# Loading q and k six rows to a partition for three batches, holding the last batch's loads back, and a new order of work

## The chip, the cores and the metric

The kernel runs on one core of one Trainium2 chip. The core has a matrix engine (TensorE, "PE" in the profile, with its weight loads as "PEld"), a vector engine (VectorE, "DVE"), a scalar engine (ScalarE, "ACT"), a general engine (GpSimd, "POOL"), a sync engine ("SP") that here only issues DMA transfers, and 16 DMA engines that all queues share. The metric is the device time of one execution in microseconds; less is better.

## The reference

The inputs are q, k, v of 4 batches, 8 heads, 768 positions and 64 columns. A flag for each head says whether it is a full causal head or a streaming head, which sees only the first 4 positions and the last 64. Then come two projections, an elementwise maximum, and a third projection.

```python
scores = scale * np.matmul(q, k.transpose(0, 1, 3, 2))
mask = np.where(retr[0, :, 0, 0, None, None], full_mask, stream_mask)
a = np.exp(scores - max); a = a / (np.sum(a, axis=-1, keepdims=True) + 1e-09)
x = np.matmul(a, v)  ->  (batch * position, 8 heads * 64)
g = np.maximum(x @ w1, x @ w2)          # 512 -> 1024
out = g @ w_out                          # 1024 -> 512, float32, 3072 rows
```

Three heads are full and five are streaming in this draw.

## The kernel before

**Tiling.** The work is cut into 8 halves, (batch, half), of 384 positions each. The heads are sorted by flag, and taken in four pairs ("FF", "FS", "SS", "SS"). For each half and pair, q and k are cast to bf16 (L774, copies at L523 and L525 into the tile `qb`), turned by TensorE into PSUM (L798, six transposes at L805), and copied to the tile `qk` (`unturn`, L810), where the rows get back their order. Scores are products of k and q (L1019) into pairs of PSUM banks; ScalarE takes the exponential (L1038) into `at`; VectorE multiplies the masks in (L1057), except in half (0,0), where a matrix product adds them (L988). TensorE then multiplies by v, with a column of ones for the sum (L1082), and `normalise` (L1090) divides (L1099, L1109) into `x`.

**The projections.** The maximum of two products is written as relu(x·(w1 − w2))·w_out + x·(w2·w_out). So before the first half can be projected, VectorE forms w1 − w2 (L1238), TensorE turns w2 (L1254) and multiplies it by w_out (L1272) into `w2o`. This needs all three weights on the chip. After that each half has 32 products at L1293, the relu at L1317 or L1319, and 36 products at L1343 into the output rows (more and narrower ones in the last tile); they are copied out (L523, L525) and stored from SP's queue (L1362).

**Loads.** Batches 0, 1 and 2 come in float32 through three slots of the tile `ld`, which batches, halves and the weights w1 and w2 take in turn; a load waits until the last reader of its slot is done. q and k of a half are one transfer each on SP's queue (L583): 128 partitions, of which each holds three consecutive rows of every head, 768 bytes a piece. v is three transfers of 128 rows (L596), in pieces of 256 bytes. The weights w1 and w2 come in two transfers each on SP's queue (L677). w_out comes in four parts on POOL's queue (L694), cast on the way, and each part is issued behind a small copy on POOL (`landed`, L693) that reads the last byte of an earlier load and so waits for it. With `PACE = 1` that is the load before the latest one in the list `LOADS`; with 0 it is the latest. `LOADS` lists the loads of batch 0 and the weights: `A` and `Av` are q with k, and v, of half (0,0), `B` and `Bv` those of (0,1), `w20` is the first half of w2, `wo0` the first quarter of w_out.

Batch 3 comes in another way: q, k and v of each head are cast by the DMA and issued from POOL (`load_pair`, L629, issues at L640), 24 transfers; q and k of a pair are then turned by a DMA transpose from SP's queue (L654).

**The order.** Each engine runs its own list of instructions in a fixed order and waits at semaphores. The lists are made when the kernel is built: the class `Order` (L133) plays the whole program through with a cost for each operation, and writes each instruction to its engine at the moment at which its play begins it. What is ready at the same time is chosen by rank (`RANK`, `FRONT`, `FRONT_STEP`, `STEP`); an operation that more than one engine can do goes where it would end first, plus a bias. TensorE takes the first ready operation by the sequence of its lists; `MARGIN` says how long an operation must have been ready before it is preferred (TQ: the transposes at L805). Until 38 us of the play, gaps on TensorE are filled with products that nobody reads (`warmer`, L513). Such a filler counts as busy in the profile. `S_AFTER` says after which pair of a half the scores of the next half may begin.

`SPLIT` names the halves whose q and k are cast, turned and copied apart ((0,0) and (0,1)). The six-row form is in the code already, and is switched off by the empty `SIX`:

```python
    def six_rows(s):
        return lds[:, s, 0:2].rearrange("p t h c -> p (t h c)").rearrange("p (h c) -> p h c", h=H)
    def rows_of(s, t):
        return six_rows(s)[64 * t:64 * t + 64]
```

Of the kernel before, what the change touches and what calls it, by code (L numbers as in the profile page):

```python
# [15 lines left out]
ACT = mybir.ActivationFunctionType  # L16
# [116 lines left out]
class Order:  # L133
# [23 lines left out]
    def pe(self, name, cost, emit, deps=(), **more):  # L157
        more.setdefault("margin", MARGIN.get(name, 0.0))
        o = self.op({"PE": cost}, emit, deps, lat=0.2, share=SHARE.get(name, 1.0), **more)
        self.lists.setdefault(name, []).append(o)  # L160
        return o
# [228 lines left out]
CAST_QK = {'POOL': 0.46, 'DVE': 0.27, 'ACT': 0.4}  # L390
CAST_V = {'POOL': 0.3, 'DVE': 0.26, 'ACT': 0.26}
RANK = {
    'cast': -1.3, 'vcast': 13.15, 'unturn': 5.85, 'mix_k': 2.0, 'mix_v': -14.6, 'exp': -3.1,
    'mask': -0.85, 'norm': -11.9, 'take_x': -1.7, 'turn': -20.3, 'w2b': -16.95, 'sub': -8.25,
    'w2t': -4.1, 'wob': -0.85, 'w2o': -5.15, 'relu': 5.25, 'load': 5.9, 'out': -10.1, 'h2': 7.5,
    'table': -10.0, 'vload': 15.45,
}
NLD = 3
NQB = 4
NQK = 8  # L400
# [7 lines left out]
PE_LISTS = ('TX', 'W', 'S', 'TK', 'TQ', 'P', 'H', 'P2', 'F')  # L408
PLACES = (0, 1, 2, 0, 1, 2, 0, 1, 2, 0, 1, 2, 0, 1, 2, 0, 1, 2, 0, 1, 2, 0)
SECOND_UP = False  # L410
LOADS = ('A', 'B', 'Av', 'wo0', 'wo1', 'w20', 'wo2', 'wo3', 'w10', 'w21', 'w11', 'Bv')
BIAS = {'DVE': 0, 'ACT': 0}
BIAS_MIX = {}
W2B_BEHIND = True
NORM = {'DVE': 0.35}
TURNED_BY_DMA = ()
DMA_TURN = 0.25
PACE = 1
W2O_EARLY = 3
X_LAST = ((0, 0),)  # L420
BIASED = ((0, 0),)
# [2 lines left out]
RING_LATE = 1.0  # L424
RING = {'SP': 3300, 'POOL': 6200, 'ACT': 4224}
SPLIT = ((0, 0), (0, 1))
SIX = ()
K_BY_ACT = False
LAST_BY_ACT = True
K_LANDS = 7.6  # L430
# [6 lines left out]
    0.22, 'six': 0.37,  # L437
}
SPARE = {}
STEP = 0.2  # L440
FF_STEP = -7.9
S_AFTER = 1
S_RUN = 2
S_REST = 1
ENTER_S = 0.1
# [2 lines left out]
COLD_UNTIL = 7.5  # L448
WARM_SHARE = 0.9
SHARE = {'S': 0.45, 'W': 0.8}  # L450
MARGIN = {'W': 0.5, 'S': 2.0, 'F': 2.0, 'TQ': 2.0}
X_MARGIN = 0.4
FRONT = (
    {'mix_k': -17.5, 'mask': 49.1, 'unturn': -40.9, 'exp': 20.1, 'vcast': 23.1, 'cast': -83.2,
    'norm': 5.9}, {'vcast': 14.2, 'unturn': -4.2, 'exp': 54.0, 'mask': 18.5, 'norm': -6.2,
    'mix_k': 18.4, 'cast': 15.9},
)
FRONT_STEP = (36.1, 8.2)
UNTURN_BIAS = ({'ACT': 0.5}, {'ACT': 0.5})
SHARED = 0.89  # L460
UP_PARTS = 2
BY_ACT = {}
V_QUEUES = ()


def tile_three_full_heads(
# [3 lines left out]
    nc = tc.nc  # L470
    B, H, S, D = q.shape
    HALF = S // 2
    NT = HALF // 128
# [13 lines left out]
    w2b = keep.tile([128, KC, d_ff], BF16, name="w2b")  # L487
    w12 = keep.tile([128, KC, d_ff], BF16, name="w12")
    w2t = keep.tile([128, FC, d_model], BF16, name="w2t")
    w2o = keep.tile([128, KC, d_model], BF16, name="w2o")  # L490
    wob = keep.tile([128, FC, d_model], BF16, name="wob")
# [11 lines left out]
    landed = keep.tile([128, 1], F32, name="landed")  # L503
# [15 lines left out]
    T = {}  # L519
# [7 lines left out]
    def rank_of(kind, b, hf, at=0):  # L527
        if b:
            return RANK[kind]
        return RANK[kind] + FRONT[hf].get(kind, 0.0) + FRONT_STEP[hf] * at  # L530

# [17 lines left out]
    number, freed, loads, later, asked = [0], {}, {}, [], []  # L549
# [20 lines left out]
    def load_half(b, hf, kinds=(0, 1, 2)):  # L570
# [4 lines left out]
        def whole(t, src):  # L575
            six = (b, hf) in SIX

# [46 lines left out]
    def staged(n):  # L624
        a = lds[:, slot_of[n // HP, 0]].rearrange("p t h c -> p (t h c)").bitcast(BF16)
        a = a.rearrange("p (g c) -> p g c", c=1536)[:, n % HP]
        return a.rearrange("p (i t h d) -> p i t h d", t=2, h=2, d=D)

    def load_pair(b, p):  # L629

        n = b * HP + p
        if p == 0:
            slot_of[b, 0], old, tenants[b] = slot()
            staged_old[b] = old
        got = {}
        for hh in range(2):
            for t, src in enumerate((q, k, v)):
                def emit(_, t=t, src=src, hh=hh):
                    to = vbs[:, n % NQK, hh, :, 0:D] if t == 2 else staged(n)[:, :, t, hh]
                    nc.gpsimd.dma_start(  # L640
                        out=to,
                        in_=src[b, bass.ds(heads[2 * p + hh], 1)].rearrange("o (i p) d -> p (o i) d", p=128),
                    )
                o = op(
                    {"POOL": CAST_ISSUE}, emit,
                    [*last_w.get(n - NQK, ())] if t == 2 else [first_w[b - 2, 1, p], *wo_in.values()],
                    data=0.197 / RATE["cast"], rank=RANK["load"], parts=768, tag=f"load{b}.{p}", port=("POOL",),
                )
                if t < 2:
                    later.append((o, staged_old[b]))  # L650
                got[t, hh] = o

        def turn_pair(_):
            nc.sync.dma_start_transpose(  # L654
                out=qks[:, n % NQK].rearrange("f t (i c) -> f (t i) c", c=128),
                in_=staged(n).rearrange("p i t h d -> p (i t h d)"),
            )
        un = op(
            {"SP": 1.7}, turn_pair, [got[t, hh] for t in range(2) for hh in range(2)] + list(last_s.get(n - NQK, ())),
            data=DMA_TURN * 4 * NT, tag=f"turn{b}.{p}", rank=RANK["turn"],  # L660
        )
        leaves(b, range(3), [un])
        return un, [got[2, 0], got[2, 1]]
# [39 lines left out]
    slot_of, tenants, bias_in, table_in, staged_old, half_old, place_of = {}, {}, [], [], {}, {}, {}  # L703
    w1_in, w2_in, wo_in, flow = {}, {}, {}, []
    for what in LOADS:
        kind, c = what[:2], int(what[2:]) if what[:1] == "w" else 0
        if what[0] in "ABCD":
# [4 lines left out]
            for n, o in enumerate(loads[(*of, kinds[-1])]):  # L712
                last = (n if kinds[-1] == 2 or of not in LONG else NT - 1) * D
                row = 64 if kinds[-1] == 1 and of in SIX else 0
                place_of[o] = row, lds[row:row + 1, slot_of[of], kinds[-1], 0, last:last + 1]
        elif kind == "wo":
            wo_in[c] = load_down(c, flow[-1 - PACE:len(flow) - PACE])
        else:
# [29 lines left out]
    last_turn, last_s, last_w = {}, {}, {}  # L748
# [21 lines left out]
    def cast_qk(n, hf, hh, lo=0, hi=2):  # L770
        b, p = first_half(n)

        def emit(e):
            if (b, hf) in SIX:  # L774
                src = six_rows(slot_of[b, hf])[:, bass.ds(heads[2 * p + hh], 1), :]
# [34 lines left out]
    def unturn(n, hf, lo=0, hi=2):  # L810
        def emit(e):
            if (n // HP, hf) in SIX:
                src = bank(("pt", n, hf, 0), BF16)[:, 0:2 * HALF]
# [66 lines left out]
    def prepare(b, hf, p):  # L880
# [7 lines left out]
        else:  # L888
# [4 lines left out]
            for hh in range(2):  # L893
                for lo, hi in ((0, 1), (1, 2)) if (b, hf) in SPLIT and (b, hf) not in SIX else ((0, 2),):
                    cs.append(cast := op(
                        dict(CAST_QK) if hi - lo == 2 else dict(CAST_V), cast_qk(n, hf, hh, lo, hi),
                        [*(o for t in range(lo, hi) for o in loads[b, hf, t]), registers, *old_qb],
                        tag=f"cast{b}.{hf}.{p}", rank=rank_of("cast", b, hf, p), port=("DVE", "POOL"),
                        bias=BIAS if b else None,
                    ))  # L900
# [8 lines left out]
            for hh in range(2) if b not in V_BY_DMA else ():  # L909
                vs.append(op(  # L910
                    dict(CAST_V), cast_v(n, hf, hh), [*loads[b, hf, 2], registers, *old_v],
                    tag=f"vcast{b}.{hf}.{p}", rank=rank_of("vcast", b, hf, p), port=("POOL", "DVE"), bias=BIAS if b else None,
                ))
# [9 lines left out]
            else:  # L923
                last_turn[n, hf], turned[n, hf] = [], []
                tq = None
                for lo, hi in ((0, 1), (1, 2)) if (b, hf) in SPLIT else ((0, 2),):
                    if tq is not None and (b, hf) in SIX:
                        un = op(
                            {"DVE": 0.08 + 0.41, "ACT": 0.065 + 0.325}, unturn(n, hf, lo, hi), [tq, *old_s],
                            frees=[key], tag=f"unturn{b}.{hf}.{p}", rank=rank_of("unturn", b, hf, p),  # L930
                            bias=None if b else UNTURN_BIAS[hf],
                        )
# [15 lines left out]
                        tag=f"unturn{b}.{hf}.{p}", rank=rank_of("unturn", b, hf, p),  # L948
                        bias=None if b else UNTURN_BIAS[hf],
                    )  # L950
# [166 lines left out]
    first_w = {}  # L1117
    x_ready, norms, x_free, xt_free, at_users, all_exps = {}, {}, {}, {}, [], {}

    def attend(b, hf):  # L1120
        group = group_of(b, hf)
        exps, done = {}, {}
        for t in range(len(group)):
# [13 lines left out]
            if b or hf:  # L1137
                deps.append(first_w[(b, 0, S_AFTER) if hf else (b - 1, 1, S_AFTER)])
            s = pe("S", cost, scores(b, hf, t), deps, claims=[(("ps", b, hf, t), 2)], tag=("S", b, hf, t))
# [25 lines left out]
        for t in range(len(group)):  # L1165
            for p in range(HP):
# [13 lines left out]
                if last:  # L1180
                    old = x_free.get(len(x_free) - NX, ())
                    r = op({"DVE": 0.12}, normalise(b, hf, p, 0), [w], tag=f"norm{b}.{hf}.{p}", rank=rank_of("norm", b, hf, p))
                    a = op(dict(NORM), normalise(b, hf, p, 1), [r, *old], tag=f"norm{b}.{hf}.{p}", rank=rank_of("norm", b, hf, p))
                    z = op(
                        dict(NORM), normalise(b, hf, p, 2), [r, *old],
                        frees=[("po", n, hf)], tag=f"norm{b}.{hf}.{p}", rank=rank_of("norm", b, hf, p),
# [112 lines left out]
    def forward(b, hf, x_deps, sub_ops, wob_ops, w2o_ops):  # L1299
        old_g = g_free.get(len(g_free) - NG, ())  # L1300
        order.shift = STEP * (2 * b + hf) + FF_STEP
        relus, users = [], []
# [75 lines left out]
    for b in range(B):  # L1378
        for hf in range(2):
# [3 lines left out]
            if b and b not in CAST_BY_DMA:  # L1383
                load_half(b, hf, [t for t in range(3) if (b, hf, t) not in loads])
            order.shift = STEP * (2 * b + hf)
            for p in range(HP):
# [3 lines left out]
            if (b, hf) > (0, 1):  # L1390
                b0, hf0 = (b, 0) if hf else (b - 1, 1)
                forward(b0, hf0, x_ready[b0, hf0], *weights)
            order.shift = STEP * (2 * b + hf)
            attend(b, hf)
# [31 lines left out]
    o = pe("P", 0.06, total, [j], claims=[("judge", 1)], margin=8.0)  # L1426
# [327 lines left out]
```

## Time and profile before

| | |
|---|---|
| median of 3 runs | 183.98 us (183.62 to 185.08) |
| profiled execution | 183.75 us |
| its span, first to last instruction | 182.1 us |
| PE busy | 173.6 us, of which fillers (L513) 13.8 |
| ACT, DVE, POOL busy | 133.9, 100.9, 41.0 us |
| moved by DMA | 32.37 MB, 178 GB/s in the mean |

The profile comes from one execution. A row of a group gives line, engine, operation, tiles and shapes, the count, then busy us and mean ns of one, then the idle time before it and what ended that. A row of the timeline or of the chain of waits begins with the start and the length in us. A row of a table by stretches gives the stretch, its length, the busy time of each engine with its count of instructions, the granted clock of TensorE, the DMA engines' share (which can pass 1.00 where packets overlap) and GB/s. Busy PE time includes pipelined overlap, so it is not PE at its peak.

### The profile page before, as it was taken

What the parts mean: (1) busy time and instruction counts of PE and PEld (TensorE: products, weight loads), DVE (VectorE), ACT (ScalarE), POOL (GpSimd) and SP (SyncE); (2) the same over time, 40 slices, a digit from 0 to 9 for tenths busy, and PEclk for the clock granted to TensorE, in tenths of its full rate; (3) what the DMA queues carried; (4) which work ended last, traced back from release to release, by engine and by line L of the source; (5) the groups of instructions that cost most, each with busy time, mean ns of one, the idle gap of its engine ahead of it and who ended that gap; (6) DMA issues with size and microseconds to landing.
All of it is one profiled execution on the core that took longest, in us unless ns stands there. A gap on an engine that the chain in (4) does not pass through costs nothing.

```text
span 182.1 us, 5021 instructions
## 1 busy us (share of the span) xinstructions
PE 173.6 (95%) x1847; PEld 107.4 (59%) x1847; DVE 100.9 (55%) x303; ACT 133.9 (74%) x295; POOL 41.0 (23%) x80
## 2 busy tenths in 40 slices
PE   7998999999998999999978999999999999999992
PEld 7955974566655757655634676455566545545561
DVE  5678984698698996739444778734467300000000
ACT  3688996588599899999689999569796614624421
POOL 6414400041105905907693000000000000000000
PEclk9999999999999999999999999999999999999998
DMA  4999999999999999999999999720142313012013
GB/s 129 334 305 224 359 200 327 315 273 312 207 285 285 304 217 220 221 211 209 133 176 169 173 219 147 170 93 0 41 118 107 89 58 115 11 58 115 0 61 121
DMA packets 72529, 32.37 MB, mean 178 GB/s; under 512 B 53938, under 2 KB 67506, under 8 KB 72498
## 3 DMA queue, kind: packets, MB, share of 16 engines
q1 hardware_dynamic: 52448, 28.45, 63.8%
q0 software_dynamic: 19904, 3.41, 25.2%
q8 instruction: 16, 0.26, 0.6%
q14 instruction: 15, 0.12, 0.2%
q10 hardware_dynamic: 146, 0.13, 0.2%
HBM read 25.17 MB, written 6.29 MB: 173 GB/s over the span
## 4 chain that ended last, share of the span: by engine, by line
PE 60%; DMA 18%; SPq 8%; ACT 7%; issue 3%; DVE 1%; ACTq 0%; DVEq 0%; POOL 0%
PE ps L1343 25%; PE ps L1293 18%; DMA ld<-in_v_dram 10%; PE ps L1019 6%; PE ps L1082 5%; DMA wob<-in_moe_w_out_dram 5%; SPq L596 5%; DMA ld<-in_k_dram 4%; PE ps L1272 4%; SPq L583 3%; ACT at L1038 2%; PE ps L805 1%; ACT vb L523 1%; ACT qk L523 1%; ACT ot L523 1%
## 5 line engine op out<-in xcount | busy, mean ns | idle before, releaser
L1038 ACT ACTIVATE at<-ps 128x512 bf16<-128x512 f32 (+2 forms) x134 | 63.8, 589 | 2.9 <-PE ps L1019 2.8
L1343 PE MATMUL ps<-wob,g 128*128 128x512 bf16 (+1 forms) x200 | 46.7, 371 | 0.0
L1293 PE MATMUL ps<-xt,w 128*128 128x384 bf16 x256 | 45.6, 326 | 0.2 <-DVE x L1109 0.2
L1293 PEld LDWEIGHTS <-w 128*128 128x128 bf16 x256 | 23.7, 98 | 15.6 <-issue 0.6
L1057 DVE TENSOR_TENSOR at<-at,tab 128x1024 bf16<-128x1024 bf16 (+5 forms) x49 | 24.1, 508 | 12.1 <-ACT at L1038 11.6
L523 ACT COPY ot<-ps 128x512 f32<-128x512 f32 (+1 forms) x23 | 13.4, 582 | 23.1 <-PE ps L1343 22.9
L1317 ACT ACTIVATE g<-ps 128x384 bf16<-128x384 f32 x52 | 25.6, 500 | 6.2 <-PE ps L1293 5.9
L1343 PEld LDWEIGHTS <-g 128*128 128x128 bf16 x200 | 18.3, 98 | 18.3 <-issue 0.2
L1343 PE MATMUL ps<-w2o,xt 128*128 128x512 bf16 (+1 forms) x100 | 24.8, 371 | 0.0
L1109 DVE TENSOR_TENSOR x<-ps,rez 128x192 f32 x64 | 22.8, 357 | 1.9 <-DVE rez L1099 0.3
L1082 PEld LDWEIGHTS <-at 128*128 128x128 bf16 x477 | 19.1, 97 | 6.7 <-issue 0.7
L1019 PE MATMUL ps<-qk 64*128 64x128 bf16 (+1 forms) x330 | 20.2, 228 | 2.1 <-DVE g L1319 0.8
L1082 PE MATMUL ps<-vb,at 128*128 128x65 bf16 x387 | 20.9, 193 | 0.4 <-ACT ot L523 0.4
L1019 PEld LDWEIGHTS <-qk 64*128 64x128 bf16 x330 | 12.4, 94 | 12.7 <-issue 9.7
L513 PE MATMUL ps<-warmer 128*128 128x128 bf16 x150 | 13.8, 251 | 1.2 <-POOL warmer L1687 1.2
L525 POOL CAST vb<-ld 128x192 bf16 x21 | 8.8, 455 | 26.4 <-DMA ld<-in_v_dram 25.4
L523 ACT COPY qk<-ps 128x768 bf16<-128x768 bf16 (+1 forms) x17 | 12.5, 771 | 2.9 <-PE ps L805 2.3
L1343 PEld LDWEIGHTS <-xt 128*128 128x128 bf16 x100 | 9.1, 98 | 8.7 <-issue 0.2
L513 PEld LDWEIGHTS <-warmer 128*128 128x128 bf16 x150 | 11.4, 116 | 1.4 <-POOL warmer L1687 1.2
L525 DVE CAST qb<-ld 128x384 bf16 (+1 forms) x30 | 9.5, 371 | 4.6 <-DMA ld<-in_k_dram 2.5
L805 PE MATMUL ps<-tab,qb 128*128 128x128 bf16 x144 | 11.2, 219 | 0.8 <-DVE qk L525 0.6
L805 PEld LDWEIGHTS <-qb 128*128 128x128 bf16 x144 | 9.1, 98 | 2.7 <-issue 0.9
(70 smaller groups left out, 157.8 us busy)
## 6 DMA issues: line engine op xcount, KB each, us to landing
out_dram<-ot SPq DMA_DIRECT2D x23, 256.0 KB, 2.1
ld<-in_q_dram SPq DMA_DIRECT2D x6, 768.0 KB, 7.9
ld<-in_k_dram SPq DMA_DIRECT2D x6, 768.0 KB, 8.2
ld<-in_v_dram SPq DMA_DIRECT2D x18, 256.0 KB, 7.5
ld<-in_moe_w_dram SPq DMA_DIRECT2D x4, 1024.0 KB, 13.4
wob<-in_moe_w_out_dram POOLq DMA_DIRECT2D x4, 256.0 KB, 9.9
ld<-in_q_dram POOLq DMA_DIRECT2D x8, 96.0 KB, 7.6
ld<-in_k_dram POOLq DMA_DIRECT2D x8, 96.0 KB, 9.0
```

The lines of the kernel that those rows point to most:

```text
L513: nc.tensor.matmul(banks[e][:, 0:128], lhsT=warm, rhs=warm, start=True, stop=True)
L523: nc.scalar.copy(out=out, in_=in_)
L525: eng[e].tensor_copy(out=out, in_=in_)
L805: nc.tensor.transpose(to[:, i], qbs[:, T["qb", n, hf] % NQB, t, i].rearrange("p h d -> p (h d)"), ident)
L1019: nc.tensor.matmul(to.rearrange("p (i c) -> p i c", c=128), lhsT=lhsT, rhs=q_of(n, i, m)[rows], start=bk not in under, stop=True, skip_gro ...
L1038: nc.scalar.activation(out=at[:, bk, 0:w], in_=bank(("ps", b, hf, t), part=bk)[:, 0:w], func=ACT.Exp, scale=scale,)
L1057: eng[e].tensor_tensor(out=at, in0=at, in1=tbl, op=ALU.mult)
L1082: nc.tensor.matmul(po[:, hh, i - NT * hf, :], lhsT=ats[:, T["at", b, hf, t] % NAT, bk, e * 128:(e + 1) * 128], rhs=rhs, start=first, stop= ...
L1109: nc.vector.tensor_tensor(out=xs[:, (2 * b + hf) % NX, :, bass.ds(heads[2 * p + hh], 1), :], in0=po[:, hh, :, 0:D].unsqueeze(2), in1=z[:, ...
L1293: nc.tensor.matmul(bank(key)[:, 0:HALF], lhsT=w[:, kc, fc * 128:(fc + 1) * 128], rhs=xts[:, (2 * b + hf) % NXT, :, kc, :], start=(kc == 0) ...
L1317: nc.scalar.activation(out=g, in_=ph, func=ACT.Relu)
L1343: nc.tensor.matmul(bank(key)[:, cols], lhsT=lhsT, rhs=(w2o if kind == "x" else wob)[:, c, cols], start=(e == 0), stop=(e == len(steps) - 1),)
```

## The change

q and k of both halves of batches 0, 1 and 2 are loaded six rows to a partition: q to partitions 0 to 63, k to 64 to 127, in pieces of 1536 bytes, 512 to a transfer instead of 1024. The bytes are the same. One cast of a head then covers q and k together (384 columns), in the halves (0,0) and (0,1) too, where there were two of 192; those halves' transposes wait for both, and still leave as two copies, one for q and one for k.

The loads of the last batch get a new dependency (`BEHIND`): the last piece of v of half (2,1). On the chip it is one small copy on POOL ahead of the first of the 24 issues, and what POOL has after it waits with it.

The order is made anew with other ranks, biases and allowances, another sequence of the first loads, `PACE` 0 and `S_AFTER` 3; `normalise` may also go to ScalarE.

```diff
 RANK = {
-    'cast': -1.3, 'vcast': 13.15, 'unturn': 5.85, 'mix_k': 2.0, 'mix_v': -14.6, 'exp': -3.1,
-    'mask': -0.85, 'norm': -11.9, 'take_x': -1.7, 'turn': -20.3, 'w2b': -16.95, 'sub': -8.25,
-    'w2t': -4.1, 'wob': -0.85, 'w2o': -5.15, 'relu': 5.25, 'load': 5.9, 'out': -10.1, 'h2': 7.5,
-    'table': -10.0, 'vload': 15.45,
+    'cast': 1.15, 'vcast': 15.65, 'unturn': 5.0, 'mix_k': 0.45, 'mix_v': -20.2, 'exp': -1.1,
+    'mask': -5.2, 'norm': -13.75, 'take_x': -6.45, 'turn': -23.55, 'w2b': -16.65, 'sub': -8.15,
+    'w2t': -7.35, 'wob': 1.75, 'w2o': -7.35, 'relu': 7.4, 'load': 4.95, 'out': -9.55, 'h2':
+    1.15, 'table': -14.3, 'vload': 12.0,
 }
...
-LOADS = ('A', 'B', 'Av', 'wo0', 'wo1', 'w20', 'wo2', 'wo3', 'w10', 'w21', 'w11', 'Bv')
-BIAS = {'DVE': 0, 'ACT': 0}
+LOADS = ('A', 'wo0', 'B', 'Av', 'wo1', 'wo2', 'w20', 'wo3', 'w21', 'Bv', 'w10', 'w11')
+BIAS = {'DVE': 1, 'ACT': 0.5}
...
-NORM = {'DVE': 0.35}
+NORM = {'DVE': 0.35, 'ACT': 0.6}
...
-PACE = 1
+PACE = 0
...
-SIX = ()
+SIX = ((0, 0), (0, 1), (1, 0), (1, 1), (2, 0), (2, 1))
...
-STEP = 0.2
-FF_STEP = -7.9
-S_AFTER = 1
+STEP = 0.15
+FF_STEP = -10.1
+S_AFTER = 3
...
-MARGIN = {'W': 0.5, 'S': 2.0, 'F': 2.0, 'TQ': 2.0}
+MARGIN = {'W': 0.5, 'S': 2.0, 'F': 0.5, 'TQ': 0.2}
...
-FRONT_STEP = (36.1, 8.2)
-UNTURN_BIAS = ({'ACT': 0.5}, {'ACT': 0.5})
+FRONT_STEP = (39.0, 7.4)
+UNTURN_BIAS = ({}, {'ACT': 1.0})
...
+BEHIND = (1, 2)
...
     def load_pair(b, p):
 
         n = b * HP + p
+        behind = loads[b - 1, BEHIND[0], BEHIND[1]][-1:] if BEHIND else []
+        for o in behind:
+            place_of[o] = 0, lds[0:1, slot_of[b - 1, BEHIND[0]], BEHIND[1], 0, NT * D - D:NT * D - D + 1]
...
                 def emit(_, t=t, src=src, hh=hh):
+                    for o in [] if T.get("last batch") else behind:
+                        row, place = place_of[o]
+                        nc.gpsimd.tensor_copy(out=landed[row:row + 1], in_=place)
+                    T["last batch"] = True
...
-                    [*last_w.get(n - NQK, ())] if t == 2 else [first_w[b - 2, 1, p], *wo_in.values()],
+                    [*behind, *(last_w.get(n - NQK, ()) if t == 2 else [first_w[b - 2, 1, p], *wo_in.values()])],
```

More of the change, by code (lines that the diff above doesn't have):

```diff
@@ L450 @@
 SHARE = {'S': 0.45, 'W': 0.8}
-MARGIN = {'W': 0.5, 'S': 2.0, 'F': 2.0, 'TQ': 2.0}
+MARGIN = {'W': 0.5, 'S': 2.0, 'F': 0.5, 'TQ': 0.2}
 X_MARGIN = 0.4
 FRONT = (
-    {'mix_k': -17.5, 'mask': 49.1, 'unturn': -40.9, 'exp': 20.1, 'vcast': 23.1, 'cast': -83.2,
-    'norm': 5.9}, {'vcast': 14.2, 'unturn': -4.2, 'exp': 54.0, 'mask': 18.5, 'norm': -6.2,
-    'mix_k': 18.4, 'cast': 15.9},
-)
-FRONT_STEP = (36.1, 8.2)
-UNTURN_BIAS = ({'ACT': 0.5}, {'ACT': 0.5})
+    {'mix_k': -6.2, 'mask': 52.7, 'unturn': -49.6, 'exp': 10.0, 'vcast': 24.8, 'cast': -61.4,
+    'norm': 14.4}, {'vcast': 24.4, 'unturn': -12.0, 'exp': 63.5, 'mask': 37.1, 'norm': -0.1,
+    'mix_k': 39.3, 'cast': 11.1},
+)
+FRONT_STEP = (39.0, 7.4)
+UNTURN_BIAS = ({}, {'ACT': 1.0})
 SHARED = 0.89
```

## The prediction, made before the changed kernel was seen

> **What bounds the kernel now.** I read the page's first lines, then a table by stretches whose cuts lie where TensorE's idle time lies, then the row of the fillers.
>
> ```profile
> span 182.1 us, 5021 instructions
> ...
> PE 173.6 (95%) x1847; PEld 107.4 (59%) x1847; DVE 100.9 (55%) x303; ACT 133.9 (74%) x295; POOL 41.0 (23%) x80
> ...
> L513 PE MATMUL ps<-warmer 128*128 128x128 bf16 x150 | 13.8, 251 | 1.2 <-POOL warmer L1687 1.2
> ```
> ```profile
> core 0: us, PE busy (x) PEld busy (x) DVE busy (x) ACT busy (x) POOL busy (x), PEclk, DMA share, GB/s
> 0.00:25.60 25.60, 23.36 (x348) 19.22 (x349) 19.68 (x71) 19.23 (x48) 9.87 (x30) 1.00 0.99 263
> 25.60:57.00 31.40, 31.40 (x338) 19.01 (x338) 23.11 (x58) 24.55 (x55) 4.93 (x9) 1.00 1.07 282
> 57.00:59.00 2.00, 1.16 (x15) 0.64 (x10) 1.97 (x7) 2.00 (x6) 1.27 (x5) 1.00 0.94 264
> 59.00:92.00 33.00, 32.82 (x393) 20.65 (x391) 23.43 (x69) 30.55 (x68) 19.76 (x31) 1.00 1.53 215
> 92.00:100.00 8.00, 6.18 (x70) 2.96 (x69) 4.35 (x12) 7.36 (x18) 5.21 (x7) 1.00 2.04 183
> 100.00:178.70 78.70, 78.63 (x699) 44.94 (x695) 28.34 (x89) 49.87 (x106) 0.00 (x0) 1.00 0.45 95
> 178.70:182.10 3.40, 0.00 (x0) 0.00 (x0) 0.00 (x0) 0.34 (x1) 0.00 (x0) 0.81 0.25 80
> ```
>
> TensorE bounds it. Without the 13.8 us of fillers its work is 159.8 us, which the change leaves as it is: the same transposes and products. The other 22.3 us of the span are what can move. The front holds 16.0 (13.8 of fillers, 25.60 − 23.36 = 2.2 idle). Later idle time is 0.84 at 57 to 59, 0.18 before 92, 1.82 at 92 to 100 and 0.07 after: 2.9 together. The tail after the last product is 3.4. The granted clock is 1.00 wherever PE works. So an edit pays if it brings useful work into the first 25.6 us or takes away part of the 2.9, and costs where it opens a new gap.
>
> What ends the front stands in the chain of waits and, around it, in the timeline:
>
> ```profile
> 8.45 8.19 DMA ld<-in_v_dram
> 16.64 0.05 issue
> 16.69 0.12 POOL landed L693
> 16.82 8.71 DMA wob<-in_moe_w_out_dram
> 25.52 0.04 issue
> 25.56 0.59 PE ps L1272 x2
> ```
> ```profile
> 6.03 0.87 DVE L525 CAST qb<-ld 128x192 bf16 x3 [1.05 <-DMA ld<-in_q_dram]
> ...
> 8.46 1.11 ACT L523 CAST qb<-ld 128x192 bf16 x4 [0.15 <-DMA ld<-in_k_dram]
> ...
> 22.89 1.28 DVE L525 COPY w2t<-ps 128x1024 bf16<-128x1024 bf16 x2
> ...
> 24.22 1.11 PE L513 MATMUL ps<-warmer 128*128 128x128 bf16 x17
> ```
>
> The last long gap is filled by 17 products of the warmer from 24.22, while the turned w2 is ready at 24.17 (22.89 + 1.28). What is missing is w_out, issued at 16.82 behind a piece of v. Behind this the DMA engines are full: a share of 0.99 over the whole front.
>
> **The change part by part.**
>
> *w_out earlier.* With `wo0` behind the load of k of (0,0), its issue moves from 16.82 to about 8.5, and with the same 8.71 us it lands at 17.2, before 24.17. The product at L1272 can then begin 1.3 us sooner; the fillers there are 1.11. Its second quarter still waits for v, and its bytes now compete with q and k of (0,1), so the bounds are −1.3 and 0. I take −1.1. On POOL the copy and the issue go past the casts of q and k of batch 0:
>
> ```profile
> L694 POOL DMA_DIRECT2D wob<-in_moe_w_out_dram x4 | 3.1, 771 | 0.0
> ```
>
> A cast behind them on POOL waits 0.9 us (0.12 + 0.77); DVE and ACT can take it, so 0, and 0.9 at most for one pair.
>
> *Six rows to a partition.* q is there at 6.03, k at 8.46: 2.43 us for 768 KB in pieces of 768 bytes. No row shows a piece of 1536 bytes, or a load into 64 partitions. The nearest rows are the front's loads and a stretch in which mostly weights come, in pieces of 2 KB:
>
> ```profile
> 5.00:7.50 2.50, 2.50 (x32) 2.47 (x31) 1.36 (x5) 1.47 (x6) 1.21 (x3) 1.00 1.10 332
> ...
> 30.00:32.50 2.50, 2.50 (x14) 1.10 (x12) 0.29 (x1) 1.49 (x5) 0.00 (x0) 1.00 1.06 401
> ```
>
> If long pieces are the reason for 401 against 332 GB/s, a load takes 2.43 × 332 / 401 = 2.01 us, 0.42 less. Four such loads stand ahead of v and the weights: −1.7 at best. On the other side, if half the partitions meant half the rate, each would take 4.86, +9.7 for four. I take −1.0: the packet count halves, and 1536 bytes is nearer to the second row. The other end is the first rival below.
>
> [...]
>
> *q and k cast together.*
>
> ```profile
> L525 DVE COPY qk<-ps 128x384 bf16<-128x384 bf16 x13 | 6.5, 552 | 0.8 <-PE ps L805 0.6
> ...
> L525 DVE CAST qb<-ld 128x384 bf16 x18 | 6.1, 387 | 2.3 <-DMA ld<-in_k_dram 1.5 <-DMA out_dram<-ot 0.8
> ...
> L523 ACT CAST qb<-ld 128x384 bf16 x9 | 4.4, 540 | 0.0
> L523 ACT CAST qb<-ld 128x192 bf16 x15 | 4.3, 353 | 2.5 <-DMA ld<-in_q_dram 2.4 <-DMA ld<-in_k_dram 0.2
> ...
> L525 DVE CAST qb<-ld 128x192 bf16 x12 | 3.5, 347 | 2.2 <-DMA ld<-in_q_dram 1.1 <-DMA ld<-in_k_dram 1.0
> ```
>
> Two casts of 0.35 become one of 0.39 (DVE) or 0.54 (ACT); 32 casts become 16, and 11.2 us of engine time about 7.4. Against that, q's casts and four copies of 0.55 were done between 6.03 and 8.46, while k was on its way; now they stand behind k: 2.2 us over two engines, 1.1 for the last pair, and for the first about 0.2 (a longer cast and three more transposes). Half of the 3.8 saved falls on (0,0). Net +0.2, between −1 and +1.3.
>
> *v of (0,1) ahead of w1.* Two pieces of 256 KB move ahead of w1, 1.9 us at 282 GB/s. The products at L1293 begin later, those with v of (0,1) earlier; PE has no gap in 25.60 to 57.00, so one fills for the other. 0; up to +1.9 if nothing fills it.
>
> The front sums to −1.1 − 1.0 + 0.2 + 0 = −1.9.
>
> *The last batch's loads wait.* From 60 to 100 two queues share the DMA engines: SP's, and POOL's with the loads of batch 3. Below are the queues in that stretch, then a piece of the chain, then PE's longest gap after it in the timeline:
>
> ```profile
> q1 hardware_dynamic: 14997, 6.27, 83.1%
> q0 software_dynamic: 14960, 1.88, 80.2%
> ```
> ```profile
> 78.73 9.14 DMA ld<-in_v_dram
> ```
> ```profile
> 94.88 0.29 PE L1019 MATMUL ps<-qk 64*128 64x128 bf16 x4 [0.54 <-ACT qk L523]
> ```
>
> q0 moves 1.88 MB for as much DMA time as q1 needs for 6.27. The last v of batch 2 takes 9.14 us, lands at 87.87, and ScalarE's backlog behind it makes the gaps at 94 to 100. With q0 silent that v should land sooner; from this 1.82 I take −1.2, and −0.3 from the 0.84 at 57 to 59, which ends on a load of k too. Bounds 0 and −2.7.
>
> The new copy itself is short (0.12 to 0.2, as `landed` above). What waits behind it on POOL are the 24 issues, any casts after them, then SP's transposes at L654, and TensorE. The groups of issues, the times to landing, and the scores of (3,0) in PE's timeline, its first pair and its third:
>
> ```profile
> L640 POOL DMA_DIRECT2D ld<-in_k_dram x8 | 6.8, 849 | 0.0
> L640 POOL DMA_DIRECT2D ld<-in_q_dram x8 | 6.7, 837 | 0.0
> L640 POOL DMA_DIRECT2D vb<-in_v_dram x8 | 6.7, 834 | 7.4 <-issue 6.5 <-DMA ld<-in_q_dram 0.7
> ```
> ```profile
> ld<-in_q_dram POOLq DMA_DIRECT2D x8, 96.0 KB, 7.6
> ...
> qk<-ld SPq DMA_TRANSPOSE x4, 9.5
> ```
> ```profile
> 109.98 0.51 PE L1019 MATMUL ps<-qk 64*128 64x128 bf16 x12
> ...
> 122.02 0.23 PE L1019 MATMUL ps<-qk 64*128 64x128 bf16 x2
> ```
>
> The issues sum to 20.2 us. If v lands at 82, the first pair is there at 82 + 3.4 (four issues) + 7.6 + 9.5 = 102.5, and the last at 119.3, in time. If it lands at 88 as now, it is 108.5 and 125.3: the last pair 3.3 past the third pair's 122.0. Even then products of earlier halves can fill PE. I take 0; up to +3.3.
>
> *The new order.* Its price can't be read from rows. The old one leaves 2.9 us of gaps after the front. In the new one the transposes L805 go ahead when ready for 0.2 us instead of 2.0, so a load that lands later than planned stops PE more easily; and 16 groups of them follow loads in batches 1 and 2. Bounds 0 and +4; I take half the old gaps again, +1.4. A cast sent to POOL rather than DVE or ACT, or a norm sent to ACT, I take as 0: PE has other work there; ACT, 92% busy at 59 to 100, is the risk within the +4. `S_AFTER` keeps the next half's scores back by two pairs; while projections are there to fill PE it costs nothing, and where ScalarE runs dry by it that is in the +4 too. The tail stays.
>
> **Sum.** −1.9 − 1.5 + 0 + 1.4 = −2.0: a span of 180.1, the profiled execution 183.75 − 2.0 = 181.75. The median lies 0.23 above that execution: **182.0**.
>
> **The rivals.**
>
> *Half the partitions, half the rate* (0.20). The mechanism is the 64-partition load: from one load's +2.43 on, every load behind it is late, in a front where the DMA is full. If only A's two loads show, and B's hide behind work on (0,0): 182.0 + 1.0 + 4.9 = 187.9; if all four do, 192.7. The profile can't exclude it, since nothing before has that shape. Against it: q and k follow each other in one queue and together fill all partitions.
>
> *The new order stalls* (0.20). A load 0.25 us late at each of the 16 groups gives +4, so 182.0 − 1.4 + 4 = 184.6, and 186.1 if the 1.5 at 57 to 100 isn't won either. For it: the gaps at 92 to 100 arise that way, with the larger allowance. Against it: the DMA has less to do.
>
> *The last batch is late* (0.08). +3.3 on PE without the gain of 1.2: 186.5. Against it: PE has 78.63 of 78.70 us filled after 100, with projections left to pull ahead.
>
> *The front doesn't move* (0.05), because w1 comes last anyway: 183.9, no change.
>
> *The forecast* (0.47): 179.5 to 184.5.
>
> **Chances.** About 1% is what a measurement of this kernel can tell from no change: 182.1 and 185.8. Faster: 0.27 of the forecast's 0.47 and 0.01 of the stalls, 0.28. Same: 0.19 of the forecast, 0.05 of the stalls, 0.04 of the late batch, 0.05 of the unmoved front, 0.01 of the half rate, 0.34. Slower: the rest, 0.38. The range, 179.3 to 189.0, leaves out 0.04 below and the worse half of the half-rate rival above.
>
> **What would show it.** Landing of the second load at L583 before 8.4 (right) or after 10 (half rate); L1272 beginning at 24 or before; fillers under 13; the last v of batch 2 landing by 83 and no gap over 0.5 after it; the first transpose at L654 by 95 and scores of (3,0) without a wait on it. Gaps on PE that end on L805 would mean the order.

## The result: 8.7% slower, and the profile after

The changed kernel takes 201.81 us (198.97 to 202.75) against 183.8 (183.32 to 185.08) for the kernel before in the same comparison: a ratio of 1.0872 [1.078, 1.0963]. The ratio compares only the executions in the chip's faster state; two of the changed kernel's four (202.59 and 202.75) were in a slower one, and the medians take in all. The profiled execution took 201.03 us. All line numbers from about L630 on stand 8 higher than before (L1272 is now L1280, L805 is L813), those ahead of it 1 higher (L583 is L584).

The page of the changed kernel: its first lines, the granted clock in 40 slices, TensorE's row of fillers, and the median time from issue to landing of the loads of k (8.2 before).

```profile
span 199.4 us, 4993 instructions
...
PE 178.9 (90%) x1826; PEld 110.4 (55%) x1846; DVE 94.3 (47%) x269; ACT 141.5 (71%) x335; POOL 50.6 (25%) x101
...
PEclk9957999999999998799699999999999999999999
...
L514 PE MATMUL ps<-warmer 128*128 128x128 bf16 x149 | 12.5, 252 | 1.3 <-POOL warmer L1695 1.2
...
ld<-in_k_dram SPq DMA_DIRECT2D x6, 768.0 KB, 10.7
```

The span grew by 17.3 (199.4 − 182.1). TensorE's idle time went from 8.5 (182.1 − 173.6) to 20.5 (199.4 − 178.9): 12.0 of it. The other 5.3 is busy time: without fillers 166.4 (178.9 − 12.5) where it was 159.8, for the same products. The stretches say where. The cuts are those of the table of before, with four short ones of the front between (length, busy time of PE, PEld, DVE, ACT, POOL with counts, granted clock, DMA share, GB/s):

```profile
core 0: us, PE busy (x) PEld busy (x) DVE busy (x) ACT busy (x) POOL busy (x), PEclk, DMA share, GB/s
0.00:25.60 25.60, 20.45 (x245) 16.49 (x247) 13.43 (x50) 13.26 (x29) 8.35 (x24) 0.87 1.01 223
5.00:7.50 2.50, 2.50 (x32) 2.50 (x31) 0.95 (x4) 0.00 (x0) 0.77 (x2) 1.00 1.10 223
10.00:12.50 2.50, 1.04 (x10) 1.04 (x11) 1.58 (x5) 1.52 (x4) 1.21 (x2) 0.53 1.10 225
12.50:15.00 2.50, 2.50 (x23) 1.88 (x23) 1.67 (x3) 1.70 (x5) 0.00 (x0) 0.50 1.10 226
15.00:17.50 2.50, 2.50 (x28) 1.10 (x27) 0.00 (x0) 2.08 (x4) 0.00 (x0) 0.60 1.17 207
25.60:57.00 31.40, 27.58 (x351) 18.25 (x350) 22.50 (x57) 25.08 (x59) 4.58 (x12) 1.00 1.07 236
57.00:100.00 43.00, 35.55 (x374) 21.50 (x378) 23.30 (x60) 31.93 (x73) 20.92 (x47) 0.92 1.04 192
100.00:195.90 95.90, 95.08 (x867) 54.19 (x875) 35.02 (x104) 70.84 (x176) 16.71 (x21) 1.00 0.83 112
```

Two things are to be seen. At 5.00 to 7.50 the DMA engines are as full as before (share 1.10 in both) but move 223 GB/s instead of 332. And the idle time is new in every stretch that still has loads of the first three batches: 5.15 to 25.60 (2.24 before), 3.82 to 57 (0.00 before, where PE was busy for all of 31.40), 7.45 to 100 (2.84 before); after that 0.82.

The chain of waits stands on loads in each of those stretches, three of k and one of v (start, length, what):

```profile
3.06 14.85 DMA ld<-in_k_dram
...
45.68 10.08 DMA ld<-in_v_dram
...
65.59 10.75 DMA ld<-in_k_dram
...
84.57 6.97 DMA ld<-in_k_dram
```

The timeline of the front shows the first pair of loads coming late, and what that does to TensorE:

```profile
10.91 1.58 DVE L526 CAST qb<-ld 128x384 bf16 x5 [4.77 <-DMA ld<-in_k_dram]
...
11.46 0.82 PE L813 MATMUL ps<-tab,qb 128*128 128x128 bf16 x6 [3.56 <-ACT qb L524]
```

q and k of (0,0) are there at 10.9; before, k was there at 8.46. PE stands for 3.56 us, from 7.90 on, and the granted clock is 0.53, 0.50 and 0.60 in the three stretches from 10.00 on. In cuts of 0.1 us it falls at about 10.2, 2.3 us into the gap, and is back at 17.0.

### The profile page after: what moved, and what is told of

It is laid out like the page before. It is cut to its first block, busy times and chain, and to the rows that moved or that the text cites. A ratio compares the mean times of both kernels' runs of the same rounds, so it can differ in the third digit from the quotient of the medians.

```text
span 199.4 us, 4993 instructions
## 1 busy us (share of the span) xinstructions
PE 178.9 (90%) x1826; PEld 110.4 (55%) x1846; DVE 94.3 (47%) x269; ACT 141.5 (71%) x335; POOL 50.6 (25%) x101
## 4 chain that ended last, share of the span: by engine, by line
PE 56%; DMA 21%; SPq 7%; issue 5%; ACT 5%; POOL 3%; DVE 1%; POOLq 0%; DVEq 0%; ACTq 0%
PE ps L1351 25%; DMA ld<-in_k_dram 16%; PE ps L1301 16%; DMA ld<-in_v_dram 5%; PE ps L1090 5%; PE ps L1027 5%; SPq L584 3%; SPq L597 3%; POOL qb L526 3%; PE ps L1280 2%; ACT at L1046 2%; PE ps L813 1%; PE ps L1262 1%; PE ps L514 1%; ACT vb L524 1%
## 5 line engine op out<-in xcount | busy, mean ns | idle before, releaser
L1046 ACT ACTIVATE at<-ps 128x512 bf16<-128x512 f32 (+2 forms) x134 | 65.9, 584 | 3.3 <-PE ps L1027 3.2
L526 POOL CAST qb<-ld 128x384 bf16 x28 | 14.8, 580 | 49.3 <-DMA ld<-in_k_dram 49.3
L524 ACT COPY ot<-ps 128x512 f32<-128x512 f32 (+1 forms) x20 | 11.4, 572 | 20.3 <-PE ps L1351 19.3
L813 PE MATMUL ps<-tab,qb 128*128 128x128 bf16 x144 | 13.9, 249 | 12.1 <-ACT x L1112 3.8
L1117 DVE TENSOR_TENSOR x<-ps,rez 128x192 f32 x43 | 15.3, 356 | 10.3 <-ACT x L1112 9.4
L813 PEld LDWEIGHTS <-qb 128*128 128x128 bf16 x144 | 10.6, 113 | 15.3 <-POOL qb L526 9.8
L1112 ACT ACTIVATE x<-ps,rez 128x64 f32 x63 | 15.3, 330 | 5.3 <-DVE x L1117 2.6
L1027 PEld LDWEIGHTS <-qk 64*128 64x128 bf16 x330 | 12.5, 95 | 10.8 <-issue 9.2
L524 ACT CAST qb<-ld 128x384 bf16 x10 | 4.8, 512 | 13.6 <-DMA ld<-in_k_dram 13.6
L514 PE MATMUL ps<-warmer 128*128 128x128 bf16 x149 | 12.5, 252 | 1.3 <-POOL warmer L1695 1.2
L526 DVE COPY qk<-ps 128x384 bf16<-128x384 bf16 (+1 forms) x17 | 11.3, 689 | 4.6 <-PE ps L813 3.4
```

Of the source, the lines that this page charges most:

```text
L524: nc.scalar.copy(out=out, in_=in_)
L526: eng[e].tensor_copy(out=out, in_=in_)
L813: nc.tensor.transpose(to[:, i], qbs[:, T["qb", n, hf] % NQB, t, i].rearrange("p h d -> p (h d)"), ident)
L1027: nc.tensor.matmul(to.rearrange("p (i c) -> p i c", c=128), lhsT=lhsT, rhs=q_of(n, i, m)[rows], start=bk not in under, stop=True, skip_gro ...
L1046: nc.scalar.activation(out=at[:, bk, 0:w], in_=bank(("ps", b, hf, t), part=bk)[:, 0:w], func=ACT.Exp, scale=scale,)
L1112: nc.scalar.activation(out=xs[:, (2 * b + hf) % NX, i, bass.ds(heads[2 * p + hh], 1), :], in_=po[:, hh, i:i + 1, 0:D], func=ACT.Copy, scal ...
```

## The experiments

Three explanations stood against each other. **Which partitions:** a load into partitions 0 to 63, or 64 to 127, gets only a part of the DMA's rate. **How many:** 64 partitions, or pieces of 1536 bytes, are slow in any layout. **The order:** the new ranks and the wait of the last batch stall, and the loads only look late. A fourth came up on the way: the order is written for faster loads than come, and an order that knew it would hide them.

**The loads alone.** A kernel that issues one load after another, each followed by a copy that reads it. In outline, all in pieces of 1536 bytes (the loads in pieces of 768 bytes are left out):

```
six[0:64]    <- 768 KB of q        (partitions 0 to 63)
six[64:128]  <- the same           (64 to 127)
six[32:96]   <- the same           (32 to 95)
six[0:128:2] <- the same           (the even ones)
six          <- 1536 KB of q       (all 128)
six[0:64], six[64:128] <- q, k     (one queue; then two queues)
six[0:128:2], six[1:128:2] <- q, k (one queue)
```

> A kernel of loads alone; it leaves out the whole computation and stores zeros. Each load waits for the one before: one half of q (768 KB) into 128 partitions in pieces of 768 bytes, then in pieces of 1536 bytes into partitions 0 to 63, 64 to 127, 32 to 95, and the even ones; half of that into 64 partitions in pieces of 768 bytes; a whole batch into 128 partitions in pieces of 1536; then q and k back to back in both forms, on one queue and on two, and even with odd. In the trace of the changed kernel two loads of 768 KB took 7 to 8 us in the front, 225 GB/s. Theory 1, which partitions: 0 to 63 and 64 to 127 run at about 220 GB/s (3.6 us and a fixed 2), 32 to 95 and the even ones at 330 or more, like 128 partitions; pairs of halves serialize at 220 on one queue. Theory 2, the count of 64 partitions or the longer piece: all forms with 64 are at 220, or the whole batch in 1536-byte pieces is slow too.

Its timeline, in its third pass, where each load stood by itself. A load's time is the idle time in brackets at the copy that reads it; the issue starts some 0.03 after the copy before it ends:

```profile
127.00 0.61 SPq L42 DMA_DIRECT2D six<-in_q_dram  x1
133.64 0.15 DVE L32 COPY seen<-six 128x1 f32<-128x1 f32 x1 [6.67 <-DMA six<-in_q_dram]
133.82 0.61 SPq L44 DMA_DIRECT2D six<-in_q_dram  x1
140.14 0.15 DVE L32 COPY seen<-six 128x1 f32<-128x1 f32 x1 [6.35 <-DMA six<-in_q_dram]
...
145.43 0.15 DVE L32 COPY seen<-six 128x1 f32<-128x1 f32 x1 [5.14 <-DMA six<-in_q_dram]
...
150.70 0.15 DVE L32 COPY seen<-six 128x1 f32<-128x1 f32 x1 [5.12 <-DMA six<-in_q_dram]
...
157.66 0.15 DVE L32 COPY seen<-six 128x1 f32<-128x1 f32 x1 [6.80 <-DMA six<-in_q_dram]
...
168.00 0.15 DVE L32 COPY seen<-six 128x1 f32<-128x1 f32 x1 [10.19 <-DMA six<-in_k_dram]
...
178.02 0.15 DVE L32 COPY seen<-six 128x1 f32<-128x1 f32 x1 [9.86 <-DMA six<-in_k_dram]
...
185.47 0.15 DVE L32 COPY seen<-six 128x1 f32<-128x1 f32 x1 [7.30 <-DMA six<-in_k_dram]
```

The same 768 KB, in the same 512 pieces of 1536 bytes, into 64 partitions each time: 6.7 us into 0 to 63, 6.4 into 64 to 127, but 5.1 into 32 to 95 and 5.1 into the even ones. A whole batch of q, twice the bytes in pieces of the same 1536 bytes, takes 6.8 into all 128. So it is neither the number of partitions nor the piece. The pair of halves takes 10.2 from one queue and 9.9 from two: the second load adds 3.52 (10.19 − 6.67), and 0.786 MB / 3.52 = 223 GB/s, the rate of the front above. The even and odd pair takes 7.3; there the second adds 2.18 (7.30 − 5.12), or 361 GB/s. The 768 KB load into all 128 partitions in pieces of 768 bytes overlapped others here; its rate is read from the kernel before instead. Which 64 partitions is what decides here: the two halves at once take 0.33 us less from two queues than from one (10.19 − 9.86), while 32 to 95 and the even ones, at 5.14 and 5.12, are not held to the slow rate. Why the halves are held to it no run shows. The expectation's fixed 2 us of a load was an estimate of the author's; 6.67 − 3.52 leaves 3.15.

**The change without the six rows.**

```diff
-SIX = ((0, 0), (0, 1), (1, 0), (1, 1), (2, 0), (2, 1))
+SIX = ()
```

> The changed kernel with three rows to a partition again; everything else as changed, the order made anew for it. Theory 1 (the loads into 64 partitions are the loss): 181 to 187, k of (0,0) there at 8.4, no clock under 0.9. Theory 3 (the new ranks or the held-back loads are the loss): 195 or more.

183.13 us, 0.9949 [0.9916, 0.9981]. All of the loss is gone with this one edit. The rest of the change is no loss; it is even a gain of half a per cent against the kernel before.

**The change with q on the even and k on the odd partitions.** Same pieces, same bytes, same order of instructions; only the partitions differ, and the copies behind the transposes sort the columns accordingly. (The small copy on POOL reads two partitions, so that it waits for the same load.)

```diff
-        return six_rows(s)[64 * t:64 * t + 64]
+        return six_rows(s)[t:128:2]
...
-                src = src.rearrange("f (n t p) -> f t p n", t=2, p=64)[:, lo:hi]
+                src = src.rearrange("f (n p t) -> f t p n", t=2, p=64)[:, lo:hi]
```

> The changed kernel with q on the even partitions and k on the odd ones instead of the lower and the upper 64; the same pieces of 1536 bytes, the same order of instructions but for the copy that puts the rows back. Theory 1: each load 2.0 to 2.4 us, k of (0,0) there at 8, 180 to 187 in all. Theory 2 (64 partitions or the piece): as changed, 198 to 203. Theory 3 (order): the front mended and the total still over 190.

183.81 us, 0.9983 [0.9949, 1.0018]. Its page and its stretches:

```profile
span 182.2 us, 4993 instructions
...
PE 172.1 (94%) x1826; PEld 106.6 (59%) x1846; DVE 95.3 (52%) x269; ACT 140.2 (77%) x335; POOL 51.1 (28%) x101
```
```profile
0.00:25.60 25.60, 22.07 (x334) 18.35 (x337) 17.68 (x64) 16.54 (x37) 9.28 (x26) 1.00 1.01 283
5.00:7.50 2.50, 2.31 (x36) 2.13 (x34) 0.95 (x4) 0.00 (x0) 0.77 (x2) 1.00 1.06 392
25.60:57.00 31.40, 30.11 (x344) 18.00 (x346) 22.94 (x56) 28.15 (x69) 11.29 (x24) 1.00 0.96 268
57.00:100.00 43.00, 41.92 (x470) 25.82 (x475) 28.57 (x71) 41.17 (x105) 29.69 (x51) 1.00 1.36 202
```

The counts of instructions on every engine are those of the changed kernel (4993, 1826 on PE), and 16.3 us are gone (1.0872 − 0.9983, of 183.8). At 5.00 to 7.50 the loads run at 392 GB/s where the halves had 223 and three rows 332. The granted clock is 1.00 in all four stretches (0.87 and 0.92 in two of the changed kernel's), and the 1826 matrix instructions, fillers among them, take 172.1 instead of 178.9: the same work, so the 6.8 of busy time go with the lower clock.

**Without the wait of the last batch, and the six rows alone.** The first is the change with `BEHIND = ()`, the second the kernel before with nothing but `SIX` of the change:

```diff
-BEHIND = (1, 2)
+BEHIND = ()
```
```diff
-SIX = ()
+SIX = ((0, 0), (0, 1), (1, 0), (1, 1), (2, 0), (2, 1))
```

> The changed kernel with the last batch's loads free to go early. Theory 1: 198 to 206, the front unchanged to the instruction, as the loads into 64 partitions are still there. Theory 3 (holding back is the loss): under 192.

> The kernel before with the six-row loads for three batches and nothing else (its own ranks, sequence of loads and allowances; the order made anew with them). If the loads into half the partitions carry the loss: 195 to 204, k of (0,0) there at 10.9. If it needed the new ranks as well: under 190.

Without the wait: 200.27 us, 1.0876 [1.0798, 1.0954], the same as with it. The six rows alone: 201.7 (198.1 to 201.9) beside 183.86; the lowest of its runs is 7.7% above that. Neither the wait nor the new order has a part in the loss, and the six rows bring it in the old order too.

**Front and later batches apart.**

```diff
-SIX = ((0, 0), (0, 1), (1, 0), (1, 1), (2, 0), (2, 1))
+SIX = ((0, 0), (0, 1))
```
```diff
-SIX = ((0, 0), (0, 1), (1, 0), (1, 1), (2, 0), (2, 1))
+SIX = ((1, 0), (1, 1), (2, 0), (2, 1))
```

> The changed kernel with six rows for batch 0 alone. k of (0,0) lands 2.7 later than with all partitions and the clock falls to about 0.5 for 6.5 us (some 3 us): 188 to 191. If the front's delay is hidden by work that is there: 184.

> The changed kernel with six rows for batches 1 and 2 alone. The gaps at 50 to 100, about 10 us, and the clock of 0.83 to 0.92 there stay: 192 to 197, the front as with three rows. If those gaps came only from the late front: 184 to 186.

The four loads of batch 0 alone: 188.09, 1.0216 [1.0137, 1.0295]. The eight of batches 1 and 2 alone: 195.14, 1.0618 [1.0525, 1.0711]. Above the version without six rows (0.9949) these are 2.7% and 6.7% of 183.8, or 4.9 and 12.3 us; together 17.2, and the whole is 17.0 (1.0872 − 0.9949). The two parts add up. With the intervals of the ratios the first is 3.3 to 6.5, the second 10.5 to 14.1. By the rates of 5.00 to 7.50 a load takes 0.786 / 0.332 = 2.37 us before and 0.786 / 0.223 = 3.52 after: 1.16 more, 4.6 for four and 9.3 for eight. So the front's loss is, within its interval, its DMA time; the later eight cost theirs and some 3.0 (1.2 to 4.8) on top.

**An order that knows the rate.** The planner of the order reckons a six-row load at a rate of 0.37; the measured one is 0.22:

```diff
-    0.22, 'six': 0.37,
+    0.22, 'six': 0.22,
```

> The changed kernel with the loads as changed, but its order made with 0.22 MB per us for them instead of 0.37, which is near what the trace shows. Theory 'surprise' (most of the loss comes because the order puts work ahead that waits for late loads, and TensorE then idles and loses its clock): 186 to 193, fillers in the front and no clock under 0.9. Theory 'bytes' (12 loads longer by 1.4 each on DMA engines that are full): 197 or more.

> The changed kernel with loads as changed, an order made with 0.22 MB per us for them, and the last batch's loads free. With the wait TensorE ran full from 60 to 130 and then dry at 140 to 150, since the loads held back began at 102. If that wait hands the delay on to the end: 190 to 195. If the bytes alone set the end: 197 or more.

With it: 200.95, 1.081 [1.0677, 1.0943]; with it and without the wait: 199.62, 1.0844 [1.077, 1.0917]. The stretches of the second:

```profile
5.00:7.50 2.50, 2.50 (x49) 2.50 (x47) 0.96 (x4) 0.00 (x0) 0.78 (x2) 1.00 1.10 222
10.00:12.50 2.50, 0.84 (x14) 0.77 (x15) 1.39 (x5) 1.34 (x3) 1.18 (x2) 1.00 1.10 222
12.50:15.00 2.50, 2.18 (x34) 1.31 (x32) 1.57 (x4) 2.20 (x6) 0.53 (x2) 1.00 1.10 219
15.00:17.50 2.50, 2.50 (x37) 1.17 (x32) 0.18 (x1) 2.50 (x6) 0.00 (x0) 1.00 1.14 207
17.50:100.00 82.50, 77.52 (x942) 50.57 (x950) 53.00 (x137) 68.50 (x166) 28.41 (x56) 1.00 1.23 225
100.00:130.00 30.00, 25.60 (x209) 13.77 (x208) 10.48 (x30) 21.10 (x48) 14.26 (x25) 0.89 1.71 162
```

The clock stays at 1.00 up to 100 and TensorE is fuller until then, and still nothing is won: the idle time comes back later (4.40 at 100 to 130, with a clock of 0.89), when the work that was pulled ahead is missing. The theory that the order was merely surprised falls. With DMA engines as full as here (a share of 1.23 at 17.50 to 100) it is when the bytes come that sets the end, in both orders that were tried; neither hides the 13.9 (4.6 + 9.3) that they come late. Nor does the loss hang on the low clock in the front: this kernel, without it, is no faster.

**What is left when the loads aren't slow.** Three versions more: the kernel before with the even and odd layout alone; the change with that layout but without the wait; the change without six rows and without the wait, which leaves the new ranks and the sequence of the first loads (each by the edits shown above):

> The kernel before, with six rows for three batches on even and odd partitions and nothing else (its own ranks and sequence; the order made anew with them). The loads then run at about 375 GB/s instead of 326. If the faster loads are worth something by themselves: 181 to 183. If the data were not what held TensorE up, or q waiting for k takes the gain back: 183.5 to 186.

> The changed kernel with q on even and k on odd partitions, and the last batch's loads free to go early. If holding them back is what was won at 50 to 100: 185 or more against 183.8 with it. If it decides nothing: 183 to 184.5.

> The kernel before with the new ranks, sequence and allowances alone: three rows to a partition, the last batch's loads free. Against 183.1 with the loads held back: 184 to 186 if holding back wins 1 to 2 us, 183.1 if it decides nothing.

| | ratio to before | 95% interval |
|---|---|---|
| even and odd alone, in the old order | 0.9956 | 0.9926 to 0.9985 |
| new ranks and sequence alone | 0.9992 | 0.9968 to 1.0017 |
| the same, with the wait | 0.9949 | 0.9916 to 0.9981 |
| new ranks, even and odd, no wait | 1.0119 | 1.0061 to 1.0177 |
| the same, with the wait | 0.9983 | 0.9949 to 1.0018 |

The medians are 183.39, 184.20, 183.13, 186.69 and 183.81 us; the first lies between the two ranges that were expected for it. The wait is worth 0.4% with three rows (0.8 us, by the two intervals 0.0 to 1.5, so barely clear of none) and 1.4% with the even and odd layout (2.5 us, 1.3 to 3.7). It does relieve the DMA engines at 60 to 100, as the stretches of the change without six rows show, first with the wait and then without it (share 1.28 against 1.57):

```profile
60.00:100.00 40.00, 38.94 (x431) 23.31 (x435) 26.22 (x71) 38.03 (x96) 27.70 (x44) 1.00 1.28 193
```
```profile
25.60:57.00 31.40, 30.11 (x335) 17.77 (x338) 23.68 (x58) 28.48 (x71) 8.68 (x21) 1.00 1.08 274
60.00:100.00 40.00, 39.04 (x427) 23.55 (x431) 25.23 (x66) 38.41 (x94) 28.70 (x43) 1.00 1.57 203
```

PE's busy time there is equal, so the 0.8 do not come from the gaps at 60 to 100; where they come from isn't settled. The best two versions lie half a per cent below the kernel before, 0.9949 and 0.9956.

## Why the prediction was wrong, step by step

It said 182.0 and a range of 179.3 to 189.0; the time is 201.81. **The step that failed is "six rows to a partition":** it was put at −1.0 for the four loads of the front, and costs +17.0 for twelve. Two things were wrong in it.

*The choice between its ends.* It took the piece of 1536 bytes for what counts and 401 against 332 GB/s as the measure. That half of the reasoning is not wrong: with the even and odd layout the loads do run at 392. But these loads have a second property, partitions of the lower or the upper half only (6.7 and 6.4 us alone, against 5.1 across the middle), and for that no row of before had a price. The first rival named the load into 64 partitions, with a chance of 0.20, but not which 64; the argument against it, that q and k follow each other and together fill all partitions, is refuted by the pair's 10.2 us against 7.3.

*The number of loads.* Sum, bounds and rival all counted four loads, those of the front, though the change names six halves, twelve loads. The rival's per-load price was too high (+2.43, measured +1.16, since the rate falls to 223/332 = 0.67, not to a half), its 187.9 for the front meets what the front alone measures (188.09) by luck, with two late loads at +2.43 in place of four at +1.16, and the eight loads behind it, 12.3 of the 17.0, stood in no number. That is why even the rival ended at 192.7. The table of before had the reason to count them: the DMA share is 1.07 at 25.60 to 57.00 and 1.53 at 59 to 92, so there was no free DMA time there to hide a slower load.

The other steps, seen best where the loads aren't slow:

*w_out earlier, −1.1.* Not won with three rows. In the timeline of the change without six rows its first issue is at 8.89, as reckoned, but its first product starts at 25.78, where it was 25.56:

```profile
8.89 0.83 POOL L702 DMA_DIRECT2D wob<-in_moe_w_out_dram  x1
```
```profile
23.10 1.29 DVE L526 CAST w2b<-ld 128x1024 bf16<-128x1024 f32 x2
...
24.77 0.68 DVE L526 COPY w2t<-ps 128x1024 bf16<-128x1024 bf16 x1
...
25.78 1.04 PE L1280 MATMUL ps<-wob,w2t 128*128 128x512 bf16 x3
```

What is late next is w2: its turned copy is there at 25.45 (24.77 + 0.68), where it was 24.17. With even and odd partitions the first product starts at 24.89, 0.7 earlier than before. In the change without six rows the DMA engines have a share of 0.98 over the first 25.60 us; w_out is issued 7.9 earlier there than before (16.82 − 8.89), and the turned w2 comes 1.3 later (25.45 − 24.17).

*q and k cast together, +0.2.* Not tried by itself; with even and odd in the old order, loads and casts together come to 0.9956, −0.8 us (−1.4 to −0.3). That is the −1.0 and +0.2 of the prediction, but partly by luck: the sum was for the four loads of the front, the run has twelve, and the two terms weren't taken apart.

*The last batch's loads wait, −1.5.* The sign is right, the size 0.8 with three rows and 2.5 with even and odd; under the slow loads nothing. With three rows it didn't come where it was put, in the gaps at 57 to 100 (above); with even and odd it did for the most part, as TensorE is busy for 38.98 of the 40.00 us at 60 to 100 with the wait and for 37.04 without it, at a clock of 1.00 in both.

*Its lateness, 0.* In the changed kernel POOL's copy, behind POOL's own casts, comes at 96.41 and the first transpose of the last batch at 106.20; v by 83 and the transpose by 95 were to show the step right:

```profile
96.41 0.64 POOL L645 COPY landed<-ld 1x1 f32<-1x1 f32 x1
```
```profile
106.20 3.77 SPq L662 DMA_TRANSPOSE qk<-ld  x1
```

Yet PE is busy for 95.08 of 95.90 after 100: the projections do fill in, and the 0 holds. In the even and odd version the copy is at 78.53.

*v of (0,1) ahead of w1, 0, and the new order, +1.4.* New ranks and sequence together, without loads and wait, are 0.9992 [0.9968, 1.0017], between −0.6 and +0.3 us, where −1.1 + 1.4 were put. As the prediction feared the order moves gaps: 25.60 to 57.00 has 1.29 idle in this version (31.40 − 30.11, in the last stretches shown), where it had none. The waits of PE on L813 in the changed kernel were not its doing:

```profile
PE ps L813 <- ACT x L1112: 3.8, 2, 2.6
PE ps L813 <- ACT qb L524: 3.6, 1, 3.6
PE ps L813 <- POOL qb L526: 3.5, 4, 2.1
```

"Gaps on PE that end on L805 would mean the order", the prediction said; L805 is L813 here. These three sum to 10.9 us, and shrink to 1.8 with the even and odd layout, in an unchanged order:

```profile
PE ps L813 <- ACT qb L524: 1.5, 1, 1.5
...
PE ps L813 <- ACT qk L524: 0.3, 1, 0.3
```

A gap on a line says which work was missing, not whether its order or its data was late. Another sign, fillers under 13, came true (12.5) in a kernel that lost 17 us, as idle time took the fillers' place (5.15 in the front, 2.24 before).

It stays open where the 3.0 or so come from that the later eight loads cost above their DMA time. The clock is low there too (0.92 at 57 to 100), but no run took the clock away and left the loads.

## What to carry to other kernels

Here a layout that gave two tensors the lower and the upper half of the partitions had its loads run at 223 GB/s; on even and odd partitions the same bytes in the same pieces ran at 392, and a single load across the middle, 32 to 95, was as quick as one into the even ones (5.14 and 5.12 us). When a rival prices an operation, count every instruction of that form in the change, not those of the stretch that one happens to be looking at; and ask in each stretch whether the resource has room, which the DMA share of the profile before (1.07 and 1.53 here) says ahead of any run.

## What the runs showed of the hardware that was not expected

A load into 64 partitions was not slow as such: 5.1 us into 32 to 95 or into every second one, against 6.4 to 6.7 into either half. A second issuing queue made little of a difference to the halves (9.9 against 10.2). Pieces of 1536 bytes on alternating partitions moved at 392 GB/s at 5.00 to 7.50, where 768-byte pieces on all 128 had 332. And a single wait of TensorE of 3.56 us went with half the clock from 10.2 to 17.0, though TensorE was busy again from 11.46 on. In the change without the wait of the last batch TensorE was busy for 6.35 of the first 10 us, against 6.72 in the changed kernel, yet the mean clock from 10 to 20 was the higher one, 0.83 against 0.66. With the order that knows the rate and without the wait, where TensorE stood for 2.3 us in all ahead of the products at L813, behind casts on ACT, the clock was 1.00 from 10.00 to 17.50.
